# Tiles 2 and 3 of an attention-and-experts kernel fetched behind tiles 0 and 1, and the two column halves of each expert block copied one by one

## The chip, the cores and the metric

One Trainium2 chip, one of its cores. The metric is the device time of one execution in microseconds (us): three executions of the kernel before took 607.54, 608.6 and 610.81, so 608.6 is its median. One more execution was profiled; it took 608.95, and 607.2 of this lies between the first and the last instruction (the span). The other 1.75 us lie outside the span.

## The reference

```python
# q, k, v: (2, 8, 576, 64); w1: (E, 512, 1024), w2: (E, 1024, 512)
scores = scale * (q_chunk @ k_chunk.T)          # chunks of 64 tokens
attn = softmax(scores);  x = (attn @ v_chunk)    # 1152 tokens of 512 numbers
logits = x @ w_gate;  expert_idx = argmax(logits)   # 8 experts, one for each token
# every expert takes its first `capacity` tokens (288), in order
y[e] = relu(disp[e] @ w1[e]) @ w2[e]
x = gate_w * y[expert_idx, pos]                  # dropped tokens: zero
# then four domains: every token through every domain's pair of layers
out = sum over d of domain_probs[:, d] * (relu(x @ w1[d]) @ w2[d])   # probabilities normalised
```

## The kernel before, in words

The kernel has three stages, one behind the other. Matrix products in 32-bit keep their accuracy by splitting a number into a high part, rounded to the engine's faster format, and a low part, the remainder: ACT writes the high part (`part_hi`, L117), DVE subtracts it and writes the low part (`part_lo`, L121), and PE multiplies high by high, low by high and high by low.

**Attention (the loop at the end of the first part, nine tiles of 128 tokens).** Tile `i` has keys, queries and values side by side in one buffer `kqv[i]` (six buffers). `fetch(i)` asks for them on SP's queue: tile 0 in three pieces, every other tile in one of 768 KB. `put_k` scales the keys into a block pattern `kb`, one half on ACT (L167), the other on DVE (tile 0, and both halves of tile 1) or on POOL; `put_v` copies the values into `vb` on DVE (L175). A turn `j` of the loop does the scores of tile `j` on PE (L207), the transposed weights of tile `j-1` (L221, with ACT's copy `et`, L223), the maximum (`mx`, L213, DVE) and the exponentials (L216, ACT) of tile `j`, the values of `j-1` (L229), and for older tiles the gate's logits and the rank of each token within its expert. All engines run their instructions in the order in which the program has them, so an instruction that waits holds up what stands behind it on its engine. SP issues all plain transfers in program order; they share eight semaphores in rotation, so that a transfer also waits for the eighth before it. `warm` (L139) is a product whose result is not used.

**Experts (`block` and `expert`).** With this input six experts get tokens. The tokens of an expert are gathered with POOL's indirect transfers (`gather`, L403), by windows: window 0 and 1 have 128 rows, window 2 has 64. `block(k, w)` runs window `w` of the expert through both layers: `first` (pg, L591), ACT's copy `hs` (L606), transposes (L597, or L595 for the small block), `ht` in a high part by ACT (L613) and a low part by DVE (L614), `second` (y, L591), the copy `yr` of the result (ACT, L648, two halves of 256 columns), its transposes (L597 or L595), and the write-back of the high and low parts into `x2` (`hi_lo`, ACT L540 and DVE L541; for a large block in two pieces). The last rows of the second layer's weights are multiplied by column halves, so that `y` is finished one half after the other. Which blocks run is decided by counts from the data: (0,1), (0,0); (1,1), (1,2), (1,0); (2,0); (3,2), (3,0); (4,2), (4,0); (5,0), where (k,w) is expert and window; that is eight large and three small blocks. The branches of L700, L717, L718 and L771 around them are taken by every engine.

In the last block of an expert, (k,0), the lists `also[0..6]` put further work between its steps: the high and low parts of the next expert's weights and the next expert's transposed tokens (`xprep`, L540, L541, L544). What does not find a place there, `late(k)` does at the start of the next expert. A weight set of an expert is four buffers of two halves each: `hls[0]`, `hls[2]` belong to the first layer and `hls[1]`, `hls[3]` to the second. For the first expert `places` (L461 to L469) also computes which experts follow; SP reads that (L560) and only then asks for expert 1's weights.

**Domains (`dense`).** The two layers of the four domains follow, all tokens through each, with their products at L811, L840 and L859.

## Time and profile before

| | us |
|---|---|
| median of three executions | 608.6 |
| profiled execution | 608.95 |
| its span | 607.2 |
| PE busy | 575.0 |
| DVE busy | 297.5 |
| ACT busy | 201.0 |
| POOL busy | 68.1 |

A row of the timeline has the start in us, the length of a run of like instructions, the engine, the line of the kernel, the operation, what it writes and reads, and in brackets how long the engine stood idle before it and what ended that. "DVEq L700" as a releaser is DVE's own sequencer at the branch of L700. PE is idle for 32 us of the span; the domains begin at 229.09, and most of its idle time lies ahead of them.

### The profile page before, as it was taken

What the parts mean: (1) busy time and instruction counts of PE and PEld (TensorE: products, weight loads), DVE (VectorE), ACT (ScalarE), POOL (GpSimd) and SP (SyncE); (2) the same over time, 40 slices, a digit from 0 to 9 for tenths busy, and PEclk for the clock granted to TensorE, in tenths of its full rate; (3) what the DMA queues carried; (4) which work ended last, traced back from release to release, by engine and by line L of the source; (5) the groups of instructions that cost most, each with busy time, mean ns of one, the idle gap of its engine ahead of it and who ended that gap; (6) DMA issues with size and microseconds to landing.
All of it is one profiled execution on the core that took longest, in us unless ns stands there. A gap on an engine that the chain in (4) does not pass through costs nothing.

```text
span 607.2 us, 9022 instructions
## 1 busy us (share of the span) xinstructions
PE 575.0 (95%) x3453; PEld 505.1 (83%) x3453; DVE 297.5 (49%) x584; ACT 201.0 (33%) x402; POOL 68.1 (11%) x63
## 2 busy tenths in 40 slices
PE   6998989998898989999999999999999999999995
PEld 3785767776676769999999999999999999989984
DVE  4898856157454675243453353353363363354222
ACT  4785264277363773012212211211211211211110
POOL 3321906001101140000000000000000000000032
PEclk8999999999999998999999999999999999999999
DMA  8781298138636495100120120120220000000022
GB/s 310 278 302 68 72 307 281 51 137 285 221 131 192 151 282 183 63 0 6 66 69 1 70 69 2 70 70 1 70 70 1 1 1 0 1 1 1 1 80 82
DMA packets 17324, 61.38 MB, mean 101 GB/s; under 512 B 2720, under 2 KB 2864, under 8 KB 16624
## 3 DMA queue, kind: packets, MB, share of 16 engines
q1 hardware_dynamic: 14544, 52.95, 25.3%
q0 software_dynamic: 2720, 7.66, 4.2%
q8 instruction: 34, 0.56, 0.4%
q14 instruction: 26, 0.21, 0.1%
HBM read 55.86 MB, written 4.75 MB: 100 GB/s over the span
## 4 chain that ended last, share of the span: by engine, by line
PE 60%; issue 1%; POOL 0%; POOLq 0%; DVE 0%
PE pg L811 31%; PE po L840 20%; PE po L859 8%; POOL out L504 0%; PE po L874 0%; POOLq L961 0%; DVE xr L847 0%; POOLq L915 0%; POOLq L504 0%
## 5 line engine op out<-in xcount | busy, mean ns | idle before, releaser
L811 PE MATMUL pg<-x,hl 128*128 128x384 f32 (+1 forms) x1152 | 190.1, 325 | 2.2 <-DVEq L771 2.2
L811 PEld LDWEIGHTS pg<-x,hl 128*128 128x128 f32 x1152 | 187.0, 189 | 3.6 <-issue 2.4
L840 PE MATMUL po<-hl,h 128*128 128x512 f32 (+1 forms) x588 | 134.6, 387 | 0.0
L840 PEld LDWEIGHTS po<-hl,h 128*128 128x128 f32 x588 | 108.3, 188 | 22.2
L121 DVE TENSOR_TENSOR hl<-raw,hl 128x1024 fp32r<-128x1024 f32 x80 | 95.3, 1219 | 23.1 <-ACT hl L117 21.3
L821 ACT ACTIVATE h<-pg 128x384 fp32r<-128x384 f32 x64 | 31.5, 492 | 187.8 <-PE pg L811 186.0
L822 DVE SCALAR_TENSOR_TENSOR h<-pg,h 128x384 fp32r<-128x384 f32 x64 | 35.7, 558 | 95.9 <-ACT h L821 95.9
L117 ACT CAST hl<-raw 128x1024 fp32r<-128x1024 f32 x80 | 81.6, 1058 | 2.0 <-DMA raw<-in_w_all 1.1
L591 PE MATMUL pg<-hl,xt 128*128 128x512 f32 x240 | 61.9, 402 | 6.5 <-issue 2.9
L591 PE MATMUL y<-hl,ht 128*128 128x512 f32 (+1 forms) x300 | 63.4, 357 | 4.1 <-DVE ht L614 3.9
L591 PEld LDWEIGHTS y<-hl,ht 128*128 128x128 f32 x300 | 47.4, 188 | 15.6 <-DVE ht L614 8.7
L847 DVE SCALAR_TENSOR_TENSOR xr<-po,mcol,xr 128x512 f32<-128x512 f32 (+1 forms) x43 | 31.7, 738 | 57.6 <-PE po L840 55.2
L591 PEld LDWEIGHTS pg<-hl,xt 128*128 128x128 f32 x240 | 43.2, 188 | 17.8 <-issue 6.9
L859 PE MATMUL po<-h,hl 128*128 128x288 f32 x384 | 52.5, 296 | 0.0
L859 PEld LDWEIGHTS po<-h,hl 128*128 128x128 f32 x384 | 51.9, 188 | 0.0
L818 ACT CAST h<-pg 128x288 fp32r<-128x288 f32 x32 | 12.8, 400 | 97.0 <-DVE pg L816 97.0
L403 POOL DMA_INDIRECT xr<-x_d,gidx x24 | 25.2, 1050 | 119.3 <-PEq L700 92.6
L868 POOL MEMSET raw<- 128x512 f32 x1 | 0.5, 527 | 270.6 <-DVE hl L121 270.6
L865 DVE TENSOR_TENSOR rest<-po,rest 128x288 f32<-128x288 f32 x28 | 12.8, 458 | 27.1 <-PE po L859 27.1
L816 DVE SCALAR_TENSOR_TENSOR pg<-pg,xt 128x288 f32<-128x288 f32 x32 | 22.3, 697 | 1.7 <-PE pg L811 1.7
L819 DVE TENSOR_TENSOR h<-pg,h 128x288 fp32r<-128x288 f32 x32 | 14.7, 458 | 15.4 <-ACT h L818 15.4
L541 DVE TENSOR_TENSOR x<-tp,x 128x256 f32 (+1 forms) x19 | 8.1, 425 | 25.8 <-ACT x L540 25.2
(168 smaller groups left out, 398.1 us busy)
## 6 DMA issues: line engine op xcount, KB each, us to landing
raw<-in_w_all SPq DMA_DIRECT2D x72, 512.0 KB
kqv<-in_kqv SPq DMA_DIRECT2D x8, 768.0 KB
raw<-in_w_all SPq DMA_DIRECT2D x4, 1024.0 KB
x_d<-x SPq DMA_DIRECT2D x9, 256.0 KB
xt<-meta_d SPq DMA_DIRECT2D x1, 1056.0 KB
kqv<-in_kqv SPq DMA_DIRECT2D x3, 256.0 KB
xr<-x_d,gidx POOLq DMA_INDIRECT x24
cc<-in_cst SPq DMA_DIRECT2D x1, 373.5 KB
```

What stands on the lines that cost most here:

```text
L117: nc.scalar.copy(hls[j][:, 0, a:b], raws[j][:, a:b])
L121: nc.vector.tensor_tensor(out=hls[j][:, 1, a:b], in0=raws[j][:, a:b], in1=hls[j][:, 0, a:b].bitcast(F32), op=ALU.subtract)
L403: nc.gpsimd.indirect_dma_start(out=xrs[k % 2][0:n, w, :], out_offset=None, in_=x_d[:, :], in_offset=bass.IndirectOffsetOnAxis(ap=ix, axis=0))
L591: nc.tensor.matmul(o, t(a), wt(b), start=start and i == 0, stop=stop and i == len(pairs) - 1, skip_group_check=True)
L811: nc.tensor.matmul(pg[:, 0:n], w1(u % 2, a, kd)[:, ff * P:ff * P + P], x2[:, b, kd, g * GW:g * GW + n], start=c == 0, stop=c == 3 * KD - 1)
L816: nc.vector.scalar_tensor_tensor(out=hs, in0=hs, scalar=0.0, in1=domain(u // NH), op0=ALU.max, op1=ALU.mult)
L819: nc.vector.tensor_tensor(out=h[:, ff, 1, 0:n], in0=hs, in1=h[:, ff, 0, 0:n].bitcast(F32), op=ALU.subtract)
L821: nc.scalar.activation(out=h[:, ff, 0], in_=pg[:, 0:GW], func=ACTF.Relu)
L822: nc.vector.scalar_tensor_tensor(out=h[:, ff, 1], in0=pg[:, 0:GW], scalar=0.0, in1=h[:, ff, 0].bitcast(F32), op0=ALU.max, op1=ALU.subtract)
L840: nc.tensor.matmul(po, h[:, ff, a, tt * P:tt * P + P], w2(u % 2, b, ff)[:, cols], start=c == 0, stop=c == 3 * NF - 1)
L847: nc.vector.scalar_tensor_tensor(out=acc[t][:, cols], in0=po, scalar=pe, in1=acc[t][:, cols], op0=ALU.mult, op1=ALU.add)
L859: nc.tensor.matmul(po[:, 0:W], w2(u % 2, b, ff)[:, d * P:d * P + P], h[:, ff, a, 0:W], start=c == 0, stop=c == 3 * NF - 1)
```

## The change

1. **Fetches at the start.** Tile 1 is asked for in three pieces, as tile 0. Ahead of the requests for tiles 2 and 3 POOL copies one element into their buffers, which reads tile 0's values and tile 1's keys: SP's request waits for that copy. The rest of `cst`, `wg` and `dp` are asked for between tiles 2 and 3. In turn 0 the maximum of tile 0 stands ahead of the copies of its values and of `ones` on DVE.
2. **Gather.** Four one-element memsets on POOL into the `x` buffers stand ahead of the first gather; they take over the waits for the stores from these buffers.
3. **`ht`** has its own two buffers for each block size (`h64`, `h128`).
4. **Column halves.** ACT's copy of a half of `y` into `yr` stands right behind that half's products, ahead of the other half's.
5. **Write-back.** A large block's `x2` parts are written in one piece of 512 numbers a row.
6. **Low parts.** `part_lo(1, 0)` of the next expert and the load behind it move from `late` into `also[4]` of the block before; for expert 0 `part_lo(1, 1)` moves into the block (0,1), ahead of `part_lo(3, 0)` and `places`.

```diff
--- before.py
+++ after.py
@@ -148,10 +148,13 @@
         kqv = {}
         KQV = 6
 
-        def fetch(i):
+        def fetch(i, behind=None):
             if i < NT:
                 kqv[i] = ap_.tile([P, 3, DM], F32, tag="kqv", bufs=KQV, name="kqv")
-                if i == 0:
+                if behind is not None:
+
+                    nc.gpsimd.tensor_copy(kqv[i][0:1, 0, 0:1], behind)
+                if i < 2:
                     for t in range(3):
                         nc.sync.dma_start(out=kqv[i][:, t], in_=kqv_d[:, i, t])
                 else:
@@ -178,22 +181,19 @@
         fetch(0)
         nc.sync.dma_start(out=cc[:, 0:P], in_=cst[:, 0:P])
         fetch(1)
-        fetch(2)
-        fetch(3)
-        nc.sync.dma_start(out=cc[:, P:], in_=cst[:, P:])
-        nc.sync.dma_start(out=wgs, in_=wg)
-        nc.sync.dma_start(out=dps, in_=dp)
-        for i in range(4, KQV):
-            fetch(i)
         for j, eng in enumerate((nc.vector, nc.gpsimd)):
             eng.memset(kbs[j], 0.0)
             eng.memset(vbs[j], 0.0)
             eng.memset(vbs[j][0:64, :, :, 0, D:D + 1], 1.0)
             eng.memset(vbs[j][64:128, :, :, 1, D:D + 1], 1.0)
+        fetch(2, kqv[0][0:1, 2, 0:1])
+        nc.sync.dma_start(out=cc[:, P:], in_=cst[:, P:])
+        nc.sync.dma_start(out=wgs, in_=wg)
+        nc.sync.dma_start(out=dps, in_=dp)
+        fetch(3, kqv[1][0:1, 0, 0:1])
+        for i in range(4, KQV):
+            fetch(i)
         put_k(0)
-        for f in put_v(0):
-            f()
-        nc.vector.memset(ones, 1.0)
 
         t_ps = ps.tile([P, 3, NE], F32, name="t_ps")
         d_all = sp.tile([P, NT, NE], F32, bufs=1, name="d_all")
@@ -335,6 +335,9 @@
                 x_t(c)
             rest = list(rank(d)) if d >= 0 else []
             softmax(a)
+            if j == 0:
+                weave(put_v(0))
+                nc.vector.memset(ones, 1.0)
             if j < 3:
                 for i in ((1, 2), (3,), (4,))[j]:
                     put_k(i)
@@ -390,6 +393,9 @@
         tokens(n)
 
 
+        for i in range(NT - 4, NT):
+            nc.gpsimd.memset(X[i][0:1, 0:1], 0.0)
+
         g0 = sp.tile([P, 3, NE], F32, bufs=1, name="g0")
         nc.vector.tensor_tensor(out=g0, in0=t_ps, in1=bc(oh0, 3, 1), op=ALU.mult)
         gidx0 = cp.tile([P, 3], I32, name="gidx0")
@@ -609,7 +615,7 @@
                 tp = (tps, pg0)[h][w][:, 0:NF * n].rearrange("p (f n) -> p f n", f=NF)
                 for j in range(NF):
                     turned(tp[:, j], hs[h][:, j * P:j * P + P])
-                ht[h] = hp_.tile([P, NF, 2, n], F32R, tag="h", name="ht")
+                ht[h] = hp_.tile([P, NF, 2, n], F32R, tag=f"h{n}", name="ht")
                 nc.scalar.activation(out=ht[h][:, :, 0], in_=tp, func=ACTF.Relu)
                 nc.vector.scalar_tensor_tensor(out=ht[h][:, :, 1], in0=tp, scalar=0.0, in1=ht[h][:, :, 0].bitcast(F32),
                                                op0=ALU.max, op1=ALU.subtract)
@@ -640,12 +646,11 @@
 
             second(1, range(NF - 2))
             halves = [slice(j * DM // 2, (j + 1) * DM // 2) for j in range(2)]
+            yr = hp_.tile([P, DM], F32, tag="ys", bufs=1, name="yr")
             for cols in halves:
                 second(1, range(NF - 2, NF), cols)
-            yr = hp_.tile([P, DM], F32, tag="ys", bufs=1, name="yr")
+                nc.scalar.copy(yr[:, cols], y[:, cols])
             ty = tps[w][:, 0:KD * n].rearrange("p (d n) -> p d n", d=KD)
-            for cols in halves:
-                nc.scalar.copy(yr[:, cols], y[:, cols])
             place(5)
             for d in range(KD):
                 turned(ty[:, d], yr[:, d * P:d * P + P])
@@ -654,15 +659,13 @@
                 at = nc.s_assert_within(o_r[k] + form_r[k] * P - P, 0, NTOK + 2 * P,
                                         skip_runtime_bounds_check_because="the small block is that of forms 2 and 3")
             cols = bass.ds(at, n)
-            for d in (slice(0, KD // 2), slice(KD // 2, KD)) if not both else (slice(0, KD),):
-                hi_lo(x2[:, 0, d, cols], x2[:, 1, d, cols], ty[:, d])
+            hi_lo(x2[:, 0, :, cols], x2[:, 1, :, cols], ty)
             place(6)
 
         def late(k):
 
-            for h in range(2):
-                part_lo(1, h)
-                load(k + 1, 1, h)
+            part_lo(1, 1)
+            load(k + 1, 1, 1)
             for h in range(2):
                 part_hi(3, h)
                 part_lo(3, h)
@@ -689,9 +692,8 @@
                         xturn(0, kd, ts[kd], w)
                 for kd in range(KD):
                     xsplit(0, kd, ts[kd])
-                for j in (2, 1):
-                    for h in range(2):
-                        part_lo(j, h)
+                for j, h in ((2, 0), (2, 1), (1, 0)):
+                    part_lo(j, h)
                 chores = list(dense_rows())
             elif k + 2 < NE:
                 gather(k + 2)
@@ -703,8 +705,9 @@
 
                 count(1)
                 with tc.If(form_r[0] > 2) as two:
-                    block(0, 1, [[], [lambda: part_lo(3, 0)], [places], [lambda: part_lo(3, 1)], [], [], []])
+                    block(0, 1, [[], [lambda: part_lo(1, 1), lambda: part_lo(3, 0)], [places], [lambda: part_lo(3, 1)], [], [], []])
                 with two.Else():
+                    part_lo(1, 1)
                     places()
                     for h in range(2):
                         part_lo(3, h)
@@ -758,6 +761,7 @@
             nxt(5, 2)
             hi(4, 1, 0)
             hi(4, 1, 1)
+            lo(4, 1, 0)
             nxt(6, 3)
             for i in range(1, 6):
                 also[i] += chores[4 * i - 4:4 * i]
```

SP at the start, before: the first pieces of tile 0 (three), part of `cst`, tiles 1 to 3, the rest of `cst`, `wg`, `dp`, and tile 4. `DMAHW` are the eight semaphores of the transfers.

```order
L156 DMA kqv<-in_kqv 128x512 x3
L179 DMA cc<-in_cst 128x128
L158 DMA kqv<-in_kqv 128x1536 x3
L183 DMA cc<-in_cst 128x747
L184 DMA wgs<-in_wg 128x32 [waits DMAHW0_49]
L185 DMA dps<-in_dp 128x36 [waits DMAHW1_49]
L158 DMA kqv<-in_kqv 128x1536 [waits DMAHW2_49]
```

And in the change:

```order
L159 DMA kqv<-in_kqv 128x512 x3
L182 DMA cc<-in_cst 128x128
L159 DMA kqv<-in_kqv 128x512 x3
L161 DMA kqv<-in_kqv 128x1536 [waits Pool_49]
L190 DMA cc<-in_cst 128x747 [waits DMAHW0_49]
L191 DMA wgs<-in_wg 128x32 [waits DMAHW1_49]
L192 DMA dps<-in_dp 128x36 [waits DMAHW2_49]
L161 DMA kqv<-in_kqv 128x1536 [waits DMAHW3_49,Pool_49]
```

Tile 1 is three requests now; tile 2 (the row that waits for Pool) stops the queue until POOL's copy is done, and tile 3 stands behind `dp` and waits for POOL too.

PE at the end of the block (1,1), before: the last products into `y`, then the transposes of the copied result `yr`.

```order
L591 MATMUL y<-hl_97,ht 128x512 x4
L591 MATMUL y<-hl_97,ht 128x256 x12
L597 MATMUL tp_1029<-cc,yr 128x128 [waits Activation_49]
L597 MATMUL tp_1029<-cc,yr 128x128
L597 MATMUL tp_1029<-cc,yr 128x128 [waits Activation_49]
L597 MATMUL tp_1029<-cc,yr 128x128
```

And in the change (`y` in halves of six products each):

```order
L597 MATMUL y<-hl_97,ht 128x512 x4
L597 MATMUL y<-hl_97,ht 128x256 x6
L597 MATMUL y<-hl_97,ht 128x256 [waits Activation_49]
L597 MATMUL y<-hl_97,ht 128x256 x5
L603 MATMUL tp_1037<-cc,yr 128x128 x2
L603 MATMUL tp_1037<-cc,yr 128x128 [waits Activation_49]
L603 MATMUL tp_1037<-cc,yr 128x128
```

The first product of the second half now waits for ACT, and by the semaphore's count that is for ACT's copy of the first half. The first two transposes have no wait of their own any more; the third waits for the copy of the second half. In a small block the halves are four products each.

DVE at the passage from expert 2 to expert 3, before: `hl_96`, `hl_95` and `hl_97` are the weight buffers `hls[2]`, `hls[1]` and `hls[3]`, `xt` the next expert's tokens, `x_1013` is `x2`; the two branches are L771 and L700, and the last row is the first `ht`.

```order
L541 TENSOR_TENSOR x_1013<-tp_1028,x_1013 128x2x128 [waits Activation_49]
L541 ISA
L541 TENSOR_TENSOR x_1013<-tp_1028,x_1013 128x2x128 [waits Activation_49]
L541 TENSOR_TENSOR xt_1033<-pg_1031,xt_1033 128x256 [waits Activation_49]
L771 COMPARE_AND_BRANCH
L961 BRANCH_PREFETCH_HINT
L121 TENSOR_TENSOR hl_95<-raw_91,hl_95 128x1024 [waits DMAHW0_49]
L121 TENSOR_TENSOR hl_95<-raw_91,hl_95 128x1024 [waits DMAHW1_49]
L121 TENSOR_TENSOR hl_97<-raw_93,hl_97 128x1024 [waits DMAHW2_49,Activation_49]
L121 TENSOR_TENSOR hl_97<-raw_93,hl_97 128x1024 [waits DMAHW3_49,Activation_49]
L700 COMPARE_AND_BRANCH
L614 SCALAR_TENSOR_TENSOR ht<-tp_1029,ht 128x4x128 [waits DVE_49,Activation_49]
```

And in the change (`x_1021` is `x2`), from the third low part of `also` on:

```order
L121 TENSOR_TENSOR hl_95<-raw_91,hl_95 128x1024 [waits DMAHW2_49,Activation_49]
L547 TENSOR_TENSOR xt_1041<-tp_1038,xt_1041 128x256 [waits Activation_49]
L547 ISA
L547 TENSOR_TENSOR x_1021<-tp_1036,x_1021 128x4x128 [waits Activation_49]
L547 TENSOR_TENSOR xt_1041<-pg_1039,xt_1041 128x256 [waits Activation_49]
L775 COMPARE_AND_BRANCH
L965 BRANCH_PREFETCH_HINT
L121 TENSOR_TENSOR hl_95<-raw_91,hl_95 128x1024 [waits DMAHW3_49]
L121 TENSOR_TENSOR hl_97<-raw_93,hl_97 128x1024 [waits DMAHW4_49,Activation_49]
L121 TENSOR_TENSOR hl_97<-raw_93,hl_97 128x1024 [waits DMAHW5_49,Activation_49]
L702 COMPARE_AND_BRANCH
L620 SCALAR_TENSOR_TENSOR ht<-tp_1037,ht 128x4x128 [waits Activation_49]
```

One low part of `hl_95` stands ahead of the end of the block instead of behind it, the two pieces of `x2` are one, and three low parts instead of four stand ahead of the branch of L702 (L700 before).

## Rows read from the trace of the kernel before

**Rows 1.** The page, part 1 and part 5 (busy, mean ns | idle before).

```profile
PE 575.0 (95%) x3453; PEld 505.1 (83%) x3453; DVE 297.5 (49%) x584; ACT 201.0 (33%) x402; POOL 68.1 (11%) x63
...
L121 DVE TENSOR_TENSOR hl<-raw,hl 128x1024 fp32r<-128x1024 f32 x80 | 95.3, 1219 | 23.1 <-ACT hl L117 21.3
```

**Rows 2.** Busy time by windows (us, PE, PEld, DVE, ACT, POOL, PEclk, DMA, GB/s): domains.

```profile
229.00:595.00 366.00, 365.92 (x2103) 342.90 (x2104) 151.55 (x235) 70.36 (x125) 6.39 (x7) 1.00 0.11 37
```

**Rows 3.** PE's waits: line, waited for, us in total, times, longest.

```profile
PE y L591 <- DVE ht L614: 3.9, 5, 1.1
...
PE tp L597 <- ACT yr L648: 3.0, 8, 0.8
...
PE pg L811 <- DVEq L771: 2.2, 1, 2.2
PE tp L595 <- ACT yr L648: 1.6, 3, 0.5
...
PE pg L544 <- DVEq L700: 0.7, 1, 0.7
```

**Rows 4.** Timeline of the start (start, us, engine, line, operation [idle before]).

```profile
2.61 1.38 SPq L158 DMA_DIRECT2D kqv<-in_kqv  x3
...
3.59 0.42 DVE L169 TENSOR_SCALAR kb<-kqv 64x512 f32<-64x512 f32 x1
...
6.12 0.86 DVE L175 COPY vb<-kqv 64x512 f32<-64x512 f32 x2 [2.11 <-DMA kqv<-in_kqv]
...
7.81 1.75 ACT L216 ACTIVATE e<-s_ps,mx 128x64 f32<-128x64 f32 x8 [3.58 <-DVE mx L213]
9.40 0.86 DVE L169 TENSOR_SCALAR kb<-kqv 64x512 f32<-64x512 f32 x2 [1.62 <-DMA kqv<-in_kqv]
...
10.36 0.66 PE L207 MATMUL s_ps<-kb,kqv 128*64 128x128 f32 x8 [3.75 <-DVE kb L169]
...
11.23 0.63 ACT L167 ACTIVATE kb<-kqv 64x512 f32<-64x512 f32 x1 [1.67 <-DMA kqv<-in_kqv]
11.36 1.50 POOL L169 TENSOR_SCALAR kb<-kqv 64x512 f32<-64x512 f32 x1 [8.44 <-PE et_ps L221]
...
12.77 1.92 PE L229 MATMUL o_ps<-vb,et 128*64 128x130 f32 x16
...
15.60 0.66 PE L207 MATMUL s_ps<-kb,kqv 128*64 128x128 f32 x8
...
17.94 1.11 PE L229 MATMUL o_ps<-vb,et 128*64 128x130 f32 x16
```

**Rows 5.** Windows again: the clock ahead of tile 2's scores.

```profile
11.50:14.50 3.00, 3.00 (x27) 2.46 (x25) 1.42 (x3) 1.69 (x6) 2.65 (x2) 0.50 1.06 417
```

**Rows 6.** Timeline from the first gather to the first expert's products.

```profile
56.09 0.18 DVE L397 TENSOR_REDUCE gidx<-g 128x3 int32<-128x24 f32 x1
...
57.14 1.18 POOL L403 DMA_INDIRECT xr<-x_d,gidx  x1 [19.33 <-DVE st L420]
...
63.08 0.76 DVE L541 TENSOR_TENSOR xt<-tp,xt 128x256 fp32r<-128x256 f32 x2 [0.24 <-ACT xt L540]
```

**Rows 7.** Timeline of the block (0,1) on DVE and PE's weight loads.

```profile
69.56 1.21 DVE L121 TENSOR_TENSOR hl<-raw,hl 128x1024 fp32r<-128x1024 f32 x1
...
72.23 0.69 DVE L614 SCALAR_TENSOR_TENSOR ht<-pg,ht 128x512 fp32r<-128x512 f32 x1 [0.27 <-ACT ht L613]
...
72.98 0.99 PEld L591 LDWEIGHTS y<-hl,ht 128*128 128x128 f32 x5 [0.22 <-DVE ht L614]
```

**Rows 8.** Timeline of PE in expert 1 and at the start of expert 2.

```profile
101.12 0.73 PE L591 MATMUL y<-hl,ht 128*128 128x512 f32 x2 [0.68 <-DVE ht L614]
...
108.09 0.71 PE L597 MATMUL tp<-cc,yr 128*128 128x128 f32 x4 [0.79 <-ACT yr L648]
...
119.40 1.10 PE L595 MATMUL tp<-cc,yr 128*128 128x64 f32 x8 [0.52 <-ACT yr L648]
...
138.69 2.68 PE L591 MATMUL pg<-hl,xt 128*128 128x512 f32 x11 [1.91 <-issue]
```

**Rows 9.** Timeline of the passage from expert 2 to expert 3.

```profile
151.01 0.65 ACT L648 COPY yr<-y 128x256 f32<-128x256 f32 x2 [1.05 <-PE y L591]
...
151.43 0.71 PE L597 MATMUL tp<-cc,yr 128*128 128x128 f32 x4 [0.30 <-ACT yr L648]
...
151.96 0.42 DVE L541 TENSOR_TENSOR xt<-tp,xt 128x256 fp32r<-128x256 f32 x1 [1.80 <-ACT xt L540]
...
152.81 2.11 PE L591 MATMUL pg<-hl,xt 128*128 128x512 f32 x8 [0.45 <-PEq L700]
...
153.46 0.43 DVE L541 TENSOR_TENSOR x<-tp,x 128x256 f32 x1 [0.44 <-ACT x L540]
...
154.13 4.62 DVE L121 TENSOR_TENSOR hl<-raw,hl 128x1024 fp32r<-128x1024 f32 x4
...
155.69 1.19 PE L591 MATMUL pg<-hl,xt 128*128 128x512 f32 x4 [0.76 <-issue]
...
158.92 0.38 ACT L613 ACTIVATE ht<-tp 128x256 fp32r<-128x256 f32 x1 [2.44 <-DVEq L700]
...
159.82 1.20 PE L591 MATMUL y<-hl,ht 128*128 128x512 f32 x4 [1.11 <-DVE ht L614]
```

## The prediction

> **What bounds the kernel now.** I read the page first: PE is busy for 95% of the span, every other engine for half of it or less [rows 1]. The windows then show that the domains, from 229 to 595, leave PE no gap (365.92 of 366.00 us) [rows 2]. The diff touches nothing there, so the change can only win where PE waits ahead of 229. The table of PE's waits [rows 3] and the timeline name these places: 3.75 us at the start, where PE waits for the keys of tile 1 [rows 4]; 4.6 us in eleven waits for the copies `yr` at the ends of the expert blocks (3.0 in eight, 1.6 in three); 3.9 us in five waits for the low part of `ht`; 0.7 and 2.2 us at DVE's branches. Each part of the change is aimed at one of these places, so each is followed there alone.
>
> **The start.** Tile 2's request stood in the run of three at 2.61; now it waits until tile 0's values have landed, which is 6.12, where DVE's copy of them starts [rows 4]. With a little for POOL's copy and for SP I put the request at 6.45, some 3.4 us later. In return tile 1 has the transfers to itself. Keys of tile 0 landed by 3.59 and its values by 6.12, so two pieces and a part of `cst` took 2.5 us while tiles 1 to 3 were in flight beside them; an estimate from that is 1.1 us a piece, keys of tile 1 at 7.2 and queries at 8. Before they were used at 9.40. The two `kb` copies of 0.86 then end at about 8.2, and the scores of tile 1 start at 8.3 instead of 10.36. The maximum ahead of the value copies lets ACT's exponentials start about 0.9 us (0.86 for the copies, and `ones`) ahead of 7.81.
>
> That gain is not passed on whole. On ACT the key half of tile 2 (11.23, waiting for its transfer) stands ahead of the copy `et` of tile 0, and PE's values of tile 0 (12.77) wait for that `et`. So the next limit is when tile 2 lands. It landed at 11.23 with everything ahead of it in the queue that is ahead of it now; I take 11.0, and 10.4 to 11.8 as likely ends. Tile 2's scores (15.60) also need POOL's half of its keys, 1.50 us after 11.36 [rows 4], which is no limit yet. What can be gained before 15.60 is PE's slow stretch: from 11.5 to 14.5 the granted clock is 0.50, the lower level of 1.2 GHz, after PE had been idle up to 10.36, and the sixteen values products take 1.92 us there against 1.11 at the full clock at 17.94 [rows 4, 5]. If the shorter idle time keeps the clock at 2.4 GHz, tile 2's scores come about 1.15 us earlier (0.3 by the landing, 0.8 by the products); if not, about 0.35. I take -0.8, with bounds of -2.0 (all of the 2.06 us by which tile 1's scores move) and +1.5 (tile 2 lands at 12.7).
>
> The Trainium skill, in "TensorE: Matmul & The Clock Gate", section "Part 1: The HAM clock gate", says that the slow clock is the resting state and activity lifts it. The trace agrees with the direction (0.50 behind the gap); by that rule alone the sum would take the -1.15.
>
> **The gather.** The index is written at 56.09 + 0.18 = 56.27 and the first gather starts at 57.14 [rows 6]: 0.87 us, part of which is a wait for five transfer semaphores that the memsets now take early. But the first DVE part of `xt` (63.08) followed DVE's weight work and waited for ACT for only 0.24 us [rows 6]. So -0.25, bounds 0 and -0.87.
>
> **Expert 0.** `part_lo(1,1)`, 1.21 us, now stands in (0,1) ahead of `part_lo(3,0)` (69.56), of `places` and of the second `ht` (72.23, idle only 0.27 before it) [rows 7]. `ht` comes about 0.94 later. PE's weight load, which waited 0.22 us for it, then waits about 0.75 us longer. `places` also lets SP ask for expert 1's weights, so these come about 0.5 later, on a path where DVE and the transfers are the bound until PE's wait at 101.12 [rows 8]; PE's stalls before that are swallowed there. The single write-back takes back about 0.4. I take +0.1 for all of expert 0 (bounds -0.4 and +1.2).
>
> **The column halves.** The copies come earlier, but PE's first product of the second half now waits for the copy of the first. From the last product to the first transpose the trace shows this round trip as an idle time of 0.52 us in the small block and 0.79 in (1,1) [rows 8]; with the pipeline's tail it is some 0.66 (copy begun at 151.01, transposes at 151.43 behind two others) [rows 9]. So a new stall of 0.52 to 0.66 us stands inside each of eleven blocks. At the end the old wait shrinks: two transposes (0.71 / 4 each, 0.35 together) go without a wait and cover part of the second copy. In (k,0) two further transposes cover the rest and the old 0.30 goes away; that is a net loss of 0.22 to 0.42. In a small block it is 0.52 - 0.35 = 0.17, so I take +0.2 each; in (1,1) +0.15. Had the trace's 0.52 no part to play, because ACT's copy ends before PE wants the second half, the price would be below nothing: the whole 4.6 us of old waits would come free (second rival).
>
> **The passages between experts.** From 2 to 3 DVE stands idle 1.80 us ahead of 151.96, and a low part of 1.22 us [rows 1] fits into it. Behind it DVE does the two pieces of `x2` with 0.44 us of idle between, then four low parts (154.13, 4.62 us), then the branch; ACT's `ht` waits 2.44 us for that branch, and PE's `y` 1.11 us for `ht` [rows 9]. In the change DVE has three low parts (3.46, so -1.16), the idle between the pieces is gone, and ACT's `ht`, in its own buffers, no longer waits for the branch. PE's own work ends at about 158.7 there, so all of 1.11 comes out; of the idle 0.45 and 0.76 at 152.81 and 155.69 [rows 9] I take that they swallow the half-column stall of (2,0). So -1.1, late next being PE itself. The passage from 3 to 4 has a wait for `ht` of the same size (longest 1.1 of five) [rows 3]: -1.1. From 4 to 5, where there is no small block, the 0.7 at DVE's branch of L700 [rows 3] and 0.3 of the rest of the `ht` waits go, less a little of the stall: -0.9. From 1 to 2 PE's wait is 1.91 us for "issue", nothing that a semaphore shows [rows 8]: it stays, and the stall of (1,0) adds 0.4. From 5 to the domains PE waits 2.2 us for DVE's branch [rows 3]; DVE's chain is 0.4 shorter by the single write-back and about as much later by the stall: 0.
>
> **Sum.** -0.8 (start) -0.25 (gather) +0.1 (expert 0) +0.75 (expert 1: 0.15 + 0.2 + 0.4) -1.1 -1.1 -0.9 (passages) +0.4 (two small blocks) = -2.9. The profiled execution took 608.95, so 606.05; it was 0.35 above the median of 608.6, which is what is compared, so 605.7.
>
> **The rivals.**
> *The halves cost in full.* PE pays 0.66 at each of the eleven blocks, the idle times at the passages don't swallow it, and the third transpose waits as the first did. For it: the wait is on PE, the bound, and the copy can't start before the half is finished. Against: where DVE is late anyway, PE's stall is no loss. My sum holds +0.75 in expert 1, where it would be 1.98 (+1.2), 0.4 for the two other small blocks against 1.32 (+0.9), and nothing in the three passages, in expert 0 and ahead of the domains (six blocks, +4.0): 605.7 + 6.1 = 611.8, slower than before. It decides from 0.37 us a block on: eleven times that is 4.05, which is the 1.15 that the sum already holds and the 2.9 that it wins.
> *The halves are free.* ACT's copy runs beside the second half's products. Then the waits of rows 3 for `yr` go, 4.6 us, less 0.7 in expert 0 (0.30 for (0,0), and the 0.4 that 3.0 leaves for (0,1) beside six times 0.30 and 0.79), and my stalls of 0.75 and 0.4 don't come: 605.7 - 3.9 - 1.15 = 600.7. Against: the order shows the wait on ACT.
> *Tile 2 comes as late as it is asked for.* Landing 3.4 us later (14.6) moves ACT's key half, `et` and PE's values by as much; with the slow products, tile 2's scores come about 3 us later instead of 0.8 earlier: 609.5. For it: ACT's order puts nothing ahead of this wait. Against: tile 2 landed 1.83 us after tile 1 before, so it stood in a queue behind it.
> The Trainium skill, "DMA: Bandwidth & Descriptors", section "Rules for kernel authors", says to issue a transfer early and to wait late; by that rule this rival, 609.5, would be the outcome, and no row of this trace shows a request held back.
> *The part on the start does nothing.* The keys of tile 1 are limited by the transfers' own ramp and land at 9.4 as before: 606.5.
>
> **Chances.** Forecast and its own spread (603.5 to 607.8) 0.52; halves in full 0.14; halves free 0.14; tile 2 late 0.10; start without effect 0.10. Within 0.5% of 608.6, which is 605.56 to 611.64, a measurement can hardly tell it from no change. The forecast lies at the edge, so half of its chance is faster; with the free halves 0.26 + 0.14 and a little of the fourth gives 0.43 for faster. The full halves give 0.10 of slower beyond 611.64 and a mishap at expert 0 together with a late tile 2 another 0.03; 0.44 is left for the same. For 8 in 10 the range has to reach to the edge of the second case and most of the first: 601 to 611.
>
> **What would show it.** In the profile after: PE's wait for `kb` of tile 1 down to about 1.7 us, its scores at about 8.3, values of tile 0 near 12.5; a new wait of PE's `y` for ACT's `yr`, eleven times 0.5 us, and waits of `tp` for `yr` down from 4.6 to under 2; the `ht` waits of `y` at the passages gone and ACT's `ht` without a wait for DVE's branch; the second `ht` of (0,1) about 0.9 later in its block. The domains' start moves from 229.09 to about 226.2. It is wrong if that start is at 221 (halves free) or beyond 231 (halves in full), or if tile 2's keys land later than 12.5.

## The result, and the profile after

The changed kernel took 615.38 us (median of four, 613.91 to 616.02) and the kernel before 608.07 on the same chip (median of four): ratio 1.0114, 95% interval 1.0073 to 1.0156. It is slower; 605.7 was predicted. The profiled execution took 614.78 with a span of 613.0, which is 5.8 us longer than that of before.

Most of what was aimed at was reached. PE's waits after the change (columns as in [rows 3]):

```profile
PE pg L597 <- issue: 5.5, 2, 3.1
PE y L597 <- ACT yr L652: 5.1, 10, 0.5
PE pg L815 <- ACTq L775: 4.2, 1, 4.2
PE s_ps L207 <- DVE kb L172: 1.9, 1, 1.9
...
PE y L597 <- DVE ht L620: 0.6, 1, 0.6
...
PE tp L603 <- ACT yr L652: 0.5, 2, 0.2
```

The waits for `ht` fell from 3.9 to 0.6 us, those of the transposes for `yr` from 4.6 to 0.5, and the new one of `y` for `yr` is 5.1 us in ten blocks (the eleventh, 0.52, is listed as "issue"), as forecast. What grew besides are the first and the third row: 2.9 us of "issue" became 5.5, and 2.2 us ahead of the domains became 4.2. The next rows, PE's timeline, show where, beside [rows 8] and the 0.23 that the kernel before had inside expert 5:

```profile
136.41 1.16 PE L597 MATMUL pg<-hl,xt 128*128 128x512 f32 x4 [0.66 <-PEq L720]
140.63 4.96 PE L597 MATMUL pg<-hl,xt 128*128 128x512 f32 x14 [3.07 <-issue]
...
217.33 1.77 PE L597 MATMUL pg<-hl,xt 128*128 128x512 f32 x7 [2.47 <-issue]
...
234.05 8.23 PE L815 MATMUL pg<-x,hl 128*128 128x384 f32 x30 [4.20 <-ACTq L775]
```

These are the three places at which the program jumps over whole blocks of code: expert 2 and expert 5 have neither the block of window 1 nor the small one, and behind expert 5 two experts are left out. A fourth loss is TensorE's clock. Windows of the change (us, PE, PEld, DVE, ACT, POOL, PEclk, DMA, GB/s):

```profile
26.00:28.00 2.00, 2.00 (x16) 1.92 (x18) 1.47 (x6) 1.59 (x5) 1.49 (x1) 0.50 0.51 110
...
141.00:143.00 2.00, 2.00 (x7) 1.59 (x6) 0.00 (x0) 0.00 (x0) 0.00 (x0) 0.53 0.57 172
143.00:145.00 2.00, 2.00 (x7) 1.55 (x7) 0.00 (x0) 1.09 (x2) 0.00 (x0) 0.61 0.96 252
...
234.00:236.00 2.00, 1.95 (x6) 1.98 (x7) 1.79 (x2) 1.66 (x2) 0.00 (x0) 0.50 0.03 8
236.00:238.00 2.00, 2.00 (x7) 2.00 (x7) 1.78 (x2) 0.33 (x1) 0.00 (x0) 0.50 0.33 47
238.00:240.00 2.00, 2.00 (x8) 2.00 (x8) 0.56 (x1) 0.49 (x1) 0.00 (x0) 0.50 0.66 231
```

PE runs at 1.2 GHz (a granted clock of 0.50; 0.53 and 0.61 are windows that hold a little of 2.4 GHz) behind the waits of 3.07 and 4.20 us. The kernel before had one such stretch at the start [rows 5] and a shorter one behind the domains' start; it had none in expert 2.

Stage by stage, by the starts of PE's rows in both timelines (us, after minus before; the forecast is the prediction's sum by parts, its -0.9 from expert 4 to 5 put where those waits lie, in expert 5):

| from | to | before | after | difference | forecast |
|---|---|---|---|---|---|
| start | first transposes of expert 0 | 60.71 | 61.02 | +0.31 | -1.05 |
| there | block (1,2) | 48.14 | 47.92 | -0.22 | +0.25 |
| there | expert 2 | 26.75 | 27.47 | +0.72 | +0.6 |
| there | last transposes of expert 2 | 15.83 | 18.87 | +3.04 | 0 |
| there | next small block's `y` | 8.39 | 6.73 | -1.66 | -1.1 |
| there | last transposes of expert 3 | 20.30 | 20.88 | +0.58 | +0.2 |
| there | next small block's `y` | 8.38 | 6.71 | -1.67 | -1.1 |
| there | expert 5 | 21.84 | 22.49 | +0.65 | +0.2 |
| there | last transposes of expert 5 | 15.63 | 16.70 | +1.07 | -0.9 |
| there | domains | 3.12 | 5.26 | +2.14 | 0 |
| there | end of the span | 378.11 | 378.95 | +0.84 | 0 |
| sum | | 607.2 | 613.0 | +5.80 | -2.9 |

The +3.04 in expert 2 are 1.13 of waiting, 1.59 of slow clock (the fourteen products behind the wait take 4.96 us instead of 3.37) and 0.32 for the column halves. The +0.84 of the domains arise in their first ten microseconds, at the slow clock.

### The profile page after: what moved, and what is told of

Read it like the earlier page. It is cut to its first block, busy times and chain, and to the rows that moved or that the text cites. A ratio compares the mean times of both kernels' runs of the same rounds, so it can differ in the third digit from the quotient of the medians.

```text
span 613.0 us, 9010 instructions
## 1 busy us (share of the span) xinstructions
PE 578.9 (94%) x3453; PEld 508.2 (83%) x3453; DVE 297.0 (48%) x576; ACT 201.1 (33%) x394; POOL 74.1 (12%) x69
## 4 chain that ended last, share of the span: by engine, by line
PE 59%; issue 1%; POOL 0%; POOLq 0%; DVE 0%
PE pg L815 31%; PE po L844 20%; PE po L863 8%; POOL out L510 0%; PE po L878 0%; POOLq L965 0%; DVE xr L851 0%; POOLq L919 0%; POOLq L510 0%
## 5 line engine op out<-in xcount | busy, mean ns | idle before, releaser
L597 PE MATMUL y<-hl,ht 128*128 128x512 f32 (+1 forms) x300 | 65.6, 361 | 6.3 <-ACT yr L652 5.1
L597 PE MATMUL pg<-hl,xt 128*128 128x512 f32 x240 | 63.4, 410 | 8.7 <-issue 5.5
L409 POOL DMA_INDIRECT xr<-x_d,gidx x24 | 31.4, 1310 | 99.0 <-PEq L702 86.9
L612 ACT COPY hs<-pg 128x512 f32<-128x512 f32 x22 | 13.0, 590 | 27.5 <-PE pg L597 21.6
```

The source lines that it names most:

```text
L409: nc.gpsimd.indirect_dma_start(out=xrs[k % 2][0:n, w, :], out_offset=None, in_=x_d[:, :], in_offset=bass.IndirectOffsetOnAxis(ap=ix, axis=0))
L597: nc.tensor.matmul(o, t(a), wt(b), start=start and i == 0, stop=stop and i == len(pairs) - 1, skip_group_check=True)
```

## The experiments

What code has to do with it was seen in the transfers: windows of one microsecond list one packet of a queue called "instruction" beside PE's wait in expert 2. Before, 136 to 137 us, then the change, 138 to 139 us (queue: packets, MB, share):

```profile
q1 hardware_dynamic: 24, 0.06, 15.4%
q8 instruction: 1, 0.02, 8.2%
```

```profile
q0 software_dynamic: 54, 0.19, 56.6%
q1 hardware_dynamic: 29, 0.08, 20.4%
q8 instruction: 1, 0.02, 6.0%
```

q1 carries the weights that SP has asked for. In both kernels the packet comes in the microsecond in which q1 runs dry, in the change two microseconds later (in 136 to 138 q1 still has 70.7% and 81.8%). The change asks for one transfer of 512 KB more there: the one behind `part_lo(1,0)`, which moved from behind the branch to ahead of it. That is theory Q. All ratios below are to the kernel before on the same chip, with the 95% interval; where two runs of different chips are set against each other, the text goes by these ratios or says so.

**e1: the transfer asked for late.**

```diff
             part_lo(1, 1)
             load(k + 1, 1, 1)
+            load(k + 1, 1, 0)
...
-            lo(4, 1, 0)
+            also[4].append(lambda: part_lo(1, 0))
```

> The change with one edit: part_lo(1,0) stays in also[4], but the 512 KB transfer behind it is asked for in late(), behind that of (1,1). Theory Q (the waits at the passages 1 to 2, 4 to 5 and 5 to the domains are for code, and code lands only behind the weight transfers that SP has asked for by then; the change puts one more there): PE's wait of 3.07 us in expert 2 falls to 1.9 or less, that of 2.47 in expert 5 to about 0.2 to 0.7, that of 4.20 ahead of the domains to about 2.2, and the slow clock behind them goes or shortens; 607 to 610 us, against 615.4 of the change. Rival H (the stall between the column halves makes PE late, and the code with it): the three waits stay within 0.4 us and the time at 614 to 616.

610.04 us, ratio 1.0023 (0.9993 to 1.0052). PE in expert 2 and ahead of the domains:

```profile
139.37 3.39 PE L597 MATMUL pg<-hl,xt 128*128 128x512 f32 x14 [1.30 <-issue]
...
228.29 0.93 PE L816 MATMUL pg<-x,hl 128*128 128x384 f32 x4 [3.47 <-ACTq L776]
```

The wait in expert 2 fell to 1.30 and that in expert 5 is gone; H fell. The time is at the upper edge of what Q gave. But ahead of the domains 3.47 stayed, where Q wanted 2.2.

**e2: the copies of `yr` behind both halves,** as before.

```diff
+            for cols in halves:
+                second(1, range(NF - 2, NF), cols)
             yr = hp_.tile([P, DM], F32, tag="ys", bufs=1, name="yr")
             for cols in halves:
-                second(1, range(NF - 2, NF), cols)
                 nc.scalar.copy(yr[:, cols], y[:, cols])
```

> The change with the copies of yr behind both column halves again, as before. Theory Q: ten stalls of 0.52 us go and the waits of the transposes for yr (4.6 us) come back; the code waits stay (3.1, 2.5, 4.2 within 0.5), so 613 to 615.5 us. Rival H: the code waits fall to those of before (1.9, 0.2, 2.2), 608 to 610 us.

610.42 us, 1.0023 (0.9997 to 1.0049). The code waits stayed (3.70, 2.79 and 4.20), against H, but the time fell further than the 613 to 615.5 that Q gave: by the medians the halves cost more than 2 us.

**e3: the kernel before, with the transfer early.**

```diff
-            for h in range(2):
-                part_lo(1, h)
-                load(k + 1, 1, h)
+            part_lo(1, 1)
+            load(k + 1, 1, 1)
...
             hi(4, 1, 1)
+            lo(4, 1, 0)
```

> The kernel before with part_lo(1,0) and its transfer moved from late() into also[4], for experts 0 to 5, and nothing else. Theory Q: the code waits grow as in the change (1.9 to about 3, 0.2 to about 2.3, 2.2 to about 4), which is 5 us and some slow clock, and the waits for ht at the passages (3 us) shrink by about 2: 610 to 614 us. Rival H: code waits as before, only the gain at the passages: 605 to 607 us.

610.06 us, 1.0023 (0.9996 to 1.005):

```profile
139.66 4.83 PE L591 MATMUL pg<-hl,xt 128*128 128x512 f32 x14 [3.59 <-issue]
...
215.27 1.77 PE L591 MATMUL pg<-hl,xt 128*128 128x512 f32 x7 [1.97 <-issue]
...
229.54 0.77 PE L811 MATMUL pg<-x,hl 128*128 128x384 f32 x3 [2.18 <-DVEq L771]
```

The moved low part with its transfer makes the first two waits in a kernel that has nothing else of the change, and by e1, which leaves the low part early, it is the transfer that does it. The third wait stays at 2.18, so it has another cause. The time is at the lower edge of what Q gave, and by its interval not told apart from the kernel before.

**e4: the kernel before with the change's start alone** (`fetch`, the order of the requests, the maximum, as in the change).

> The kernel before with the change's start alone (tile 1 in three pieces, tiles 2 and 3 held back, first maximum ahead of the value copies). Theory C (the low clock level that stood at 11.5 to 14.5 comes later instead, at 24.5 to 28.5 in the change, and eats the gain): tile 2's scores 1.6 us earlier, no gain left at 50 us, time within 0.5 us of the kernel before. Rival S (the low level in the change has to do with something else, and the gain lasts): 1.4 to 1.7 us faster than the kernel before.

609.41 us, 1.0014 (0.9988 to 1.0039). The scores of tile 2 start at 14.36 instead of 15.60 and expert 0's first transposes at 59.97 instead of 60.71. A stretch at the low clock lay at 137 to 141, where the kernel before had none. The time is not told apart from that of the kernel before, so S fell; C's place is wrong, since this profile has no low clock in the attention at all.

**e5: e1 and e2 together** (both diffs above).

> The change with two edits: the transfer behind part_lo(1,0) asked for in late() (as in the run with that alone), and the copies of yr behind both halves, as before. Theory: code waits and the stall between the halves are separate costs and add up. Then the stall's 5.6 us go and about 4.4 us of waits of the transposes come back, and the code waits stay at about 1.3 in expert 2, none in expert 5, 3.5 ahead of the domains: about 1 us below the run with the late transfer alone, 607 to 609.5 us. Rival: the halves are worth nothing either way (the passages swallow both), the same 610.

607.05 us, 0.9959 (0.9931 to 0.9987). By the medians it is 3 us below e1, and the intervals of the two ratios do not meet: the rival fell. The two profiled executions do not show it (spans of 606.0 and 606.5), because that of e5 had a mean granted clock of 0.984 and that of e1 one of 0.991. The wait in expert 2 is 1.91, where 1.3 was expected; ahead of the domains it is 3.48.

**e6: e5 with the transfer behind `part_lo(2,1)` late as well.**

```diff
             load(k + 1, 1, 1)
+            load(k + 1, 2, 1)
             load(k + 1, 1, 0)
...
-            lo(4, 2, 1)
+            also[4].append(lambda: part_lo(2, 1))
```

> As the run with late transfer and whole copies, with one more transfer, that behind part_lo(2,1), also moved from also[4] to late(). Theory Q: another 512 KB fewer stand ahead of the code at the three passages, so PE's code wait in expert 2 falls from about 1.3 us to under 0.3 and that ahead of the domains by 1 to 2 us: 605 to 607.5 us. Rival A: the wait ahead of the domains has nothing to do with the transfers (it is the place of ACT's code), it stays at 3.5. Rival W: the weights of the next expert but one come too late and ACT's high parts wait for them: over 609.

604.20 us, 0.9897 (0.9838 to 0.9956), from four executions. Expert 2's wait is 1.09, less of a fall than expected. In expert 5 the price of which W spoke came in, but not its time of over 609:

```profile
219.51 1.99 ACT L117 CAST hl<-raw 128x1024 fp32r<-128x1024 f32 x2 [2.96 <-DMA raw<-in_w_all]
```

ACT's high parts waited 2.96 us for weights and PE 2.27 for the `yr` behind them; behind that the wait ahead of the domains was 1.45, for DVE's branch. Since PE also came there 2.27 us late, this fall alone does not decide between Q and A.

**e7: e5 with the write-back in two pieces again** (the removed `for d in ...` of the change put back).

> As the run with late transfer and whole copies, with the write-back into x2 in two pieces again, as before (28 more instructions on ACT and on DVE each). Rival A (the wait ahead of the domains hangs on where ACT's code lies): it falls from 3.5 us for ACT's branch to 2.2 for DVE's, as in the kernel before; 606 to 609 us. Theory Q: it stays within 0.5 us of the run without this edit, and the time grows by 0 to 2 us through DVE's passages.

605.19 us, 0.9945 (0.991 to 0.9981). Ahead of the domains:

```profile
225.53 2.85 PE L818 MATMUL pg<-x,hl 128*128 128x384 f32 x9 [2.18 <-DVEq L778]
```

Rival A was right for the third wait. The time is 1.9 us below e5, with intervals that overlap.

**e8: e5 with `part_lo(1,1)` of expert 0 ahead of the block (0,1),** as before.

```diff
-                for j, h in ((2, 0), (2, 1), (1, 0)):
+                for j, h in ((2, 0), (2, 1), (1, 0), (1, 1)):
...
-   block(0, 1, [[], [lambda: part_lo(1, 1), lambda: part_lo(3, 0)], [places], ...
+   block(0, 1, [[], [lambda: part_lo(3, 0)], [places], ...
                 with two.Else():
-                    part_lo(1, 1)
```

> As the run with late transfer and whole copies, with part_lo(1,1) of expert 0 ahead of the block (0,1) again, as before. PE's wait of 0.6 us for ht in (0,1) goes, and SP asks for expert 1's weights about 0.5 to 1.2 us earlier; DVE is 1.2 us later at the first ht instead. Expected 0.3 to 0.8 us below the run without this edit; rival: none, since the first ht is late by as much.

605.9 us, 0.9948 (0.9916 to 0.998): 1.1 below e5, with intervals that overlap. The wait for `ht` in (0,1) is gone.

**e9: the kernel before with the write-back in one piece.**

```diff
-            for d in (slice(0, KD // 2), slice(KD // 2, KD)) if not both else (slice(0, KD),):
-                hi_lo(x2[:, 0, d, cols], x2[:, 1, d, cols], ty[:, d])
+            hi_lo(x2[:, 0, :, cols], x2[:, 1, :, cols], ty)
```

> The kernel before with the write-back of a large block into x2 in one piece, and nothing else (30 instructions fewer on ACT and on DVE each over the program). In the runs so far PE waited 2.2 us ahead of the domains, for DVE's branch, in all four kernels with two pieces, and 3.5 to 4.4, for ACT's branch, in five of six with one. Theory A (the one piece alone does it, by the place of ACT's code): 3.4 or more for ACT's branch here, code wait in expert 2 at 1.6 to 2.1 as before, 608 to 611 us. Rival: it needs another part of the change (buffers of ht, memsets), the wait stays at 2.2 and the time falls by 0.5 to 1.5 us.

608.49 us, 1.0003 (0.998 to 1.0025).

```profile
226.34 2.90 PE L810 MATMUL pg<-x,hl 128*128 128x384 f32 x8 [3.54 <-ACTq L770]
```

The one piece alone turns 2.2 us for DVE's branch into 3.54 for ACT's. The time of the whole kernel does not show it.

**e10: e5 with ACT's program as long as before,** counted without the instructions that only wait for a semaphore.

```diff
+        idle = cp.tile([P, 1], F16, name="idle")
+        PAD = 2
...
             hi_lo(x2[:, 0, :, cols], x2[:, 1, :, cols], ty)
+            if not both:
+                for i in range(PAD):
+                    nc.scalar.copy(idle, wz[:, 0:1])
```

> The run with late transfer, whole copies and one-piece write-back, with two one-element ACT copies that nothing reads added behind each large block's write-back: ACT has 925 instructions again (923 before, 893 with one piece). Theory L (length of ACT's code): the wait ahead of the domains falls from 3.5 to 2.2 to 2.6 us and is no longer ACT's. Rival P (the one piece itself, by when ACT arrives at the branch): it stays at 3.5 or grows by the two copies (0.4). Time 605 to 608 either way.

602.08 us, 0.9918 (0.988 to 0.9955), the lowest median of all and below the 605 to 608 expected; by its ratio it is level with e6 and e12:

```profile
221.33 3.12 PE L822 MATMUL pg<-x,hl 128*128 128x384 f32 x10 [1.84 <-DVEq L782]
```

ACT does more (sixteen copies of one element), and PE waits 1.64 us less than in e5. So rival P fell: the one piece as such is innocent, its 30 missing instructions are not. The medians differ by 5 us and the intervals of the ratios overlap. Most of the 5 us is not this wait: the executions of e10 had a mean granted clock of 0.993, those of e5 one of 0.989, an estimated 2.5 us (0.004 of 605), and up to the domains' first products e10's profile has one stretch at 1.2 GHz, e5's three.

**e11: the change with the write-back in two pieces** (as in e7).

> The change with one edit: the write-back in two pieces, as before. Theory: the wait ahead of the domains falls from 4.20 us (ACT's branch) to 2.2 to 2.9 (DVE's, the early transfer still ahead of the code), the other two code waits stay at 3.1 and 2.5 (within 0.6): 1 to 2 us below the change, and another 1 to 2 if the slow clock behind the wait shortens with it; 611.5 to 614.5. Rival (the early transfer alone makes all three): 615.

613.94 us, 1.009 (1.0058 to 1.0121). 3.27 in expert 2, 1.72 in expert 5 and 2.18 ahead of the domains: the third wait hangs on the pieces, not on the early transfer. Expert 5's fell further than expected; why is open. The time is 1.4 us below the change, with intervals that overlap.

**e12: what helped, together** (e6, with e7's and e8's edits).

> What helped, together: the change with the transfers behind part_lo(1,0) and part_lo(2,1) asked for in late(), the copies of yr behind both halves, the write-back in two pieces and part_lo(1,1) of expert 0 ahead of the block (0,1). Theory: code wait in expert 2 at about 1.1 us, none in expert 5, 2.2 or less ahead of the domains; 602 to 605 us, below the kernel before by 0.6 to 1.0%. Rival: the two late transfers reach ACT too late and cost what the code wins, 605 to 607.

604.51 us, 0.9922 (0.9873 to 0.9971). Expert 2's wait is 1.34 and the domains' 2.18. No faster than e10.

All fourteen profiles, by the two edits (us; a wait that is absent is "-"):

| | expert 2 | expert 5 | domains |
|---|---|---|---|
| transfer early (change, e2, e3, e11) | 3.07, 3.70, 3.59, 3.27 | 2.47, 2.79, 1.97, 1.72 | |
| late (before, e1, e4, e5, e7, e8, e9, e10) | 1.91, 1.30, 2.09, 1.91, 1.64, 1.91, 1.41, 1.57 | 0.23, -, -, -, 0.33, -, 0.22, - | |
| two late (e6, e12) | 1.09, 1.34 | - | |
| two pieces (before, e3, e4, e7, e11, e12) | | | 2.19, then 2.18 five times |
| one piece (change, e1, e2, e5, e8, e9) | | | 4.20, 3.47, 4.20, 3.48, 4.35, 3.54 |
| one piece, two late (e6) | | | 1.45 |
| one piece, ACT's program longer again (e10) | | | 1.84 |

Early and late do not overlap in the first two columns, nor the rows "two pieces" and "one piece" in the third; e6 and e10 are one piece too and stand apart. Two late transfers are no more than the low end of one.

**The packets' own times in the fourteen traces** tie these waits to code. In expert 2 a packet of 16 KB of the "instruction" queue q8 lands, and 1.19 to 1.48 us behind it PE goes on, in every profile, while the wait itself runs from 1.09 to 3.70 us. In expert 5 the same distance is 1.34 to 1.52 us in the seven profiles that have a wait there. Ahead of the domains it is packets of 8 KB of the "instruction" queue q14, and it is ACT that stands still first. The change, ACT's timeline, then the transfers at 231 to 232 and at 232 to 233 us:

```profile
234.34 1.99 ACT L117 CAST hl<-raw 128x1024 fp32r<-128x1024 f32 x2 [3.81 <-ACTq L775]
```

```profile
q1 hardware_dynamic: 96, 0.36, 96.3%
...
q1 hardware_dynamic: 73, 0.24, 60.3%
q8 instruction: 1, 0.02, 7.6%
q14 instruction: 2, 0.02, 3.9%
```

In the six kernels in which PE waits for ACT's branch, the first of these packets lands 1.20 to 1.40 us before PE goes on. In the six with two pieces and in e10 the last one to land ahead of ACT's branch landed 4.4 to 8.6 us before PE goes on, while expert 5 still ran, and in e6 1.90 us before. By these times both theories have a part in the third wait: with the shorter program ACT's packet comes only at the jump, and in the change it comes there, as PE's does in expert 2, when q1 runs dry.

## Why the prediction was wrong, point by point

**The passages: the step that failed.** "From 1 to 2 PE's wait is 1.91 us for 'issue', nothing that a semaphore shows [rows 8]: it stays", "From 4 to 5 ... -0.9" and "From 5 to the domains ... 0". The three waits grew by 1.16, 2.24 and 2.01 us. Expert 2, expert 5, the way into the domains and the domains' slow start were forecast at -0.9 together and took +7.09: 8.0 of the 8.7 us between the forecast and the difference of the spans. The sum moved `part_lo(1,0)` and priced DVE's 1.22 us, but not the 512 KB request that moves with it, and it took a wait without a semaphore for one that no edit can touch. e1 and e3 show the request to be the cause in experts 2 and 5, from both sides. For the third wait it is the write-back in one piece, through the length of ACT's program (e7, e9, e10, e11); I had priced the single piece as a gain of 0.4. The sign "beyond 231" came true (234.05), but not for the reason it was put down to, the halves in full.

That code is what arrives late is read from the "instruction" packets and from the jumps: PE goes on at a nearly fixed distance behind the packet in all fourteen profiles. What the packets hold, no row says. Why 30 instructions move ACT's packet from expert 5 to the jump is open; e10 shows that the number of instructions does it, for the two numbers tried.

**The slow clock** was weighed only at the start. Two new stretches, behind the longer waits, cost about 1.6 us in expert 2 and 0.8 in the domains. Where such a stretch falls differs from kernel to kernel beyond these: in the eleven profiles with the new start the first transposes of expert 0 begin anywhere from 59.1 to 63.4, earliest where no such stretch lies in the attention and latest where one lies at 14 to 17. What sets its place stays open. It also spreads the times of one and the same kernel: of the kernel before, one execution took 606.04 us at a mean granted clock of 0.993, another 612.23 at 0.986.

**The start.** Tile 1's scores at 8.65 (8.3 forecast), tile 2's key half at 10.76 (11.0), tile 2's scores 1.67 us earlier (0.8, bounds held):

```profile
6.27 0.33 SPq L161 DMA_DIRECT2D kqv<-in_kqv  x1
...
8.65 0.66 PE L207 MATMUL s_ps<-kb,kqv 128*64 128x128 f32 x8 [1.89 <-DVE kb L172]
...
10.76 0.63 ACT L170 ACTIVATE kb<-kqv 64x512 f32<-64x512 f32 x1 [2.45 <-DMA kqv<-in_kqv]
...
11.91 1.11 PE L229 MATMUL o_ps<-vb,et 128*64 128x130 f32 x16 [1.44 <-ACT et L223]
...
13.93 0.66 PE L207 MATMUL s_ps<-kb,kqv 128*64 128x128 f32 x8
```

In this one profile the rows came as forecast or better, but for tile 2 that was luck: three profiles have the old start (before, e3, e9), and they differ among themselves by more than this. The keys of tile 1 do come earlier with the new start (DVE copies them at 7.44 to 8.60 in eleven profiles, at 8.30 to 9.40 in the three). Tile 2's scores do not: the old start reaches them at 13.26, 15.03 and 15.60, the new one at 13.55 to 17.72. The earliest of all is e9, with the old start, whose granted clock is 1.00 through the attention:

```profile
10.10 0.63 ACT L167 ACTIVATE kb<-kqv 64x512 f32<-64x512 f32 x1 [1.04 <-DMA kqv<-in_kqv]
...
13.26 0.66 PE L207 MATMUL s_ps<-kb,kqv 128*64 128x128 f32 x8
```

Its first transposes of expert 0 begin at 58.51; the five new starts without a low clock in the attention (e2, e4, e7, e10, e11) have 59.14 to 59.99. Where a low clock lies in the attention, the old start has 60.36 and 60.71 and the new one 60.25 to 63.36. So the 1.67 us lie between a profile with the low clock at this place and one without it, and no run shows a gain of the new start at the end of the attention. Of the rivals, "the part on the start does nothing" has the size (e4: 1.0014, interval 0.9988 to 1.0039), though not the reason, since tile 1's keys did come earlier.

I had counted the slow stretch as removed by the shorter gap. By the Trainium skill's rule that activity lifts the slow clock ("TensorE: Matmul & The Clock Gate", "Part 1: The HAM clock gate") the shorter gap should have helped, and in the change no slow stretch followed its 1.89 us directly. In e12 one did follow a gap of the same 1.89 us (and in e6), so these runs do not bear out that the gap decides:

```profile
9.51 0.81 PE L207 MATMUL s_ps<-kb,kqv 128*64 128x128 f32 x8 [1.89 <-DVE kb L172]
...
10.00:13.00 3.00, 3.00 (x24) 2.31 (x22) 0.54 (x1) 1.10 (x2) 1.51 (x1) 0.50 1.06 417
```

The rival of the tile that lands late fell in its size: tile 2, asked for 3.2 us later (6.27 against 3.08), was used at 10.38 to 12.93, not at 14.6; with the old start it was used at 10.10, 10.85 and 11.23. By the Trainium skill's rule of asking early ("DMA: Bandwidth & Descriptors", "Rules for kernel authors") this rival should have come true; these traces do not agree, with a loss of 0.4 us by the means.

**The gather** was worth nothing: it starts 0.87 us behind the index, as before [rows 6], although its semaphore waits had been taken earlier. Forecast -0.25.

```profile
57.20 1.23 POOL L409 DMA_INDIRECT xr<-x_d,gidx  x1 [3.23 <-DVE st L426]
```

**Expert 0** was right in kind: PE waits 0.59 for `ht` in (0,1), 0.75 forecast, and it is made up for by the wait for `ht` in (0,0), 0.72 before, and by expert 1's first wait of 0.68 [rows 8], which are both gone.

**The halves** were right inside the blocks and too small in sum. PE's stall is 0.52 in each (0.46 in the first), and in the last blocks of the experts the transposes no longer wait; in (0,1) and (1,1) they wait 0.24:

```profile
181.86 0.98 PE L597 MATMUL y<-hl,ht 128*128 128x256 f32 x6 [0.52 <-ACT yr L652]
...
182.89 0.84 PE L603 MATMUL tp<-cc,yr 128*128 128x128 f32 x4
```

A small block and the large one behind it lose 0.6 us together, where I had 0.2 and 0.2 to 0.4. Over eleven blocks that is about 3.4 us (0.31 each), and the medians of e5 and e1 differ by 3.0. My sum let the passages swallow a part. The rival "halves in full" gave 611.8 by this cost alone; it came nearer to the time than the forecast, but by luck: its 0.66 a block is twice what was measured, and the waits for code, which it does not hold, made up the rest.

**From 2 to 3 and 3 to 4** the forecast was -1.1 each. From the last transposes to the small block's `y` the change takes 6.7 us instead of 8.4 (155.28 to 162.01, and 182.89 to 189.60), -1.7, or -1.3 with the half's stall ahead of it:

```profile
155.28 0.84 PE L603 MATMUL tp<-cc,yr 128*128 128x128 f32 x4
...
156.80 3.44 PE L597 MATMUL pg<-hl,xt 128*128 128x512 f32 x12 [0.45 <-PEq L702]
...
162.01 1.20 PE L597 MATMUL y<-hl,ht 128*128 128x512 f32 x4
```

## What to carry to other kernels

When work moves ahead of a branch, look at what its requests put into the transfer queues there: packets of the "instruction" queues stand among the others, and a wait of PE that the profile calls "issue", with no semaphore, can be a wait for one of them. Find the packet and the distance at which PE follows it. Such a wait is a term of the sum like any other, with a price for every transfer that is added ahead of it. Before a saved instruction is counted as a gain, ask what the shorter program does at the places where code is jumped to: here 30 instructions fewer lengthened one wait by 1.3 to 2.0 us (e9 against before, e5 against e7, the change against e11), and e10 took the wait back with copies of one element. And before a gain is read from two profiles, look at whether the slow clock lies in the stretch in one of them.

## What had not been expected of the hardware

- One transfer of 512 KB asked for before a jump makes PE's wait behind it about 1.7 us longer (3.07 to 3.70 against 1.30 to 2.09, the means of four and of eight profiles). At the 311 and 352 GB/s that the queues moved at 135 to 136 us in the change and before, 512 KB take an estimated 1.5 to 1.7 us.
- PE goes on 1.19 to 1.48 us behind the landing of an instruction packet in expert 2, in fourteen profiles, however long it has waited.
- The length of ACT's program, 893 or 925 instructions (without those that only wait for a semaphore), sets whether PE waits 3.48 us for ACT's branch or 1.84 for DVE's ahead of the same code (e5, e10); of the 32 more instructions, copies of one element that nothing reads, sixteen run.
